# Sums of the two-level products and the last fold queued behind an older joining addition

## The chip, the cores and the metric

The kernel runs on one core of a Trainium2 chip. Its five engines run independently and wait for each other on semaphores: TensorE (PE in the profile, its weight loads PEld), VectorE (DVE), ScalarE (ACT), GpSimd (POOL) and SyncE (SP, which here issues most of the DMAs). The metric is the device time of one execution in microseconds; less is better. All data are float32.

## The reference

Two stages. The first is a sparse attention over q, k and v of shape (4, 8, 768, 64): each query sees the keys nearer than 16 positions and 24 block summaries (the maximum of a block's keys, the mean of its values). The second works on the result as x of shape (4, 768, 512):

```
X = np.fft.fft(x, axis=1); X = np.fft.fft(X, axis=2)
u = x + np.real(X)
un = (u - mean(u)) / np.sqrt(var(u) + 1e-6)          # over the last axis
out = u + np.maximum(un @ w_ch1, 0.0) @ w_ch2        # 512 -> 2048 -> 512
```

## The kernel before, in words

**Batches.** The four batches (b = 0 to 3) run as a software pipeline: while the two dense layers of batch b run on PE, the attention of batch b + 1 is put between them. The change lies in the third batch (b = 2, in the code `B - 2`) and in what of the fourth (`B - 1`) runs beside it.

**Dense layers.** The hidden layer has 2048 columns, cut into eight pairs of column blocks j = 0 to 7, four to a half (c = 0 and 1). Each layer is a Strassen-like product of seven multiplications in place of eight. `gen_hidden` makes the hidden values `h` of a half, `gen_out` the second layer. In `gen_out` a row-tile i (three of them) takes seven multiplications of four matmuls each (line 1829) into three banks (ox, oy, oz), and after each a *joining addition* on DVE adds a bank into `x` (`join`, line 1832; by `tt`, line 582): seven joins to a row-tile, 21 to a half. Each join sets `marks["dense"]`, so that this mark is always the newest join. `gen_out` yields four times to a row-tile, and at each yield calls `one_sum`, which for the first half of the third batch takes two groups of `early_sums`.

**Two-level products.** For the second half of the third batch the hidden layer is not made by `gen_hidden`, but by `gen_two`, which applies the scheme at two levels: two pairs of blocks, (4, 5) and (6, 7), with seven products each, and each of the 14 products (n = 0 to 13: "11", "U2", "11+", "U3", "Z", "12", "21", twice) of seven small matmuls on 192 columns (line 1691, numbered m = 1 to 7). Matmuls of three successive products interleave. ACT copies partial results between the banks t, f and g (line 1695), the matmuls add onto the copies, and DVE adds the finished parts into `h` (`add`, line 1648); these additions are chained one behind the other by `marks["turn"]`. `start_pairs` starts this generator just before the last multiplication of `gen_out`'s first half and fills the list `started`; `gen_pairs` then runs the rest, six matmuls to a yield.

**Sums.** The products need sums of the right operand (`first_sums`, of the columns of u) and of the left one (`pair_sums` for blocks 4 and 5, `left_halves`). Those are the twelve groups in `queue["early"]`, run by `early_sums` (line 1515). The left sums of the second pair of blocks, four groups in `queue["two"]`, are taken by `gen_two` itself, one after the matmul m = 3 of a product (line 1730). They come into the tiles named vw, uu, kt, left and w in the profile.

**Fold.** Ahead of the Fourier stage of a batch its rows and columns are folded (`fold_batch`: sums and differences of x with its mirrored half). For the last batch this runs at the end of `gen_attention(3)` in 22 steps: eight for each of two parities (`par`), then six for single tokens; POOL does the small copies, memsets and additions of single rows and columns. The mirrored rows come through memory by two DMAs of POOL (`turn_tiles`, lines 1041 and 1042). What the fold gives is first read by the `y` matmuls of `gen_fourier(3)` (line 1338).

**Order.** From here on the order on each engine is not written out by hand. A planner takes the instructions in the order of the program as priorities, and issues on each engine the first that is ready by its own estimate of durations; the order is then fixed. `tc.issue_after(ins)` adds that an instruction of the same engine may be issued only behind `ins`. The order of the program comes from `drive`, which advances two generators alternately: here 44 steps of `chain(gen_hidden(2, 0), gen_out(2, 0), gen_pairs(2))` to 80 steps of `gen_attention(3)`. A yield more or less in one generator therefore shifts its later steps against the other's.

Of the kernel before, what the change touches and what calls it, by code (L numbers as in the profile page):

```python
# [496 lines left out]
def _main_program(ctx, tc, q, k, v, moe_w_ch1, moe_w_ch2, out):  # L497
# [3 lines left out]
    B, H, S, D = q.shape  # L501
# [79 lines left out]
    def tt(out, in0, in1, op):  # L581
        return nc.vector.tensor_tensor(out=out, in0=in0, in1=in1, op=op).ins  # L582
# [5 lines left out]
    nat, marks = {}, {}  # L588

    def load(b, g, *which):  # L590

        for n in which or (1, 0):
            t = nat[b, g, n] = apool.tile([P, 2, NST // 2, 2 * D], FP, tag="nat", bufs=4, name=f"{'qk'[n]}n_{b}_{g}")
            if (b, g) > (2, 0):
                t = nat[b, g, n] = t.rearrange("p e j n -> p (e j n)").rearrange("p (m c) -> p m c", c=32)
                for e in range(2):
                    for h in range(2):
                        r, o = D * e + 32 * h, (q, k)[n][b, 2 * g + e].offset + 32 * h
                        fetch(out=t[r:r + 32], in_=bass.AP((q, k)[n].tensor, o, [[D, 32], [32 * D, S // 32], [1, 32]]))
                continue  # L600
            fetch(out=t.rearrange("p e j n -> p (e j) n"),
                  in_=(q, k)[n][b, 2 * g:2 * g + 2].rearrange("e (j p s) d -> p (e j) (s d)", p=P, s=2))
# [9 lines left out]
    def block_sums(b, gg):  # L612

        heads, rows = slice(4 * gg, 4 * gg + 4), 4 * nb
        f = BLOCK // 4
        n = f * D
        vb = spool.tile([rows, D], FP, tag="vbs", bufs=2, name=f"vbs_{b}_{gg}")
        for g in (2 * gg, 2 * gg + 1):
            sums[b, g] = vb, sel[:, g % 2]
        src = v[b, heads].rearrange("h (n f) d -> (h n) (f d)", f=BLOCK)  # L620
        if done_weights:
            raw = room(f"vb_{b}_{gg}")
            raw = [raw[0:rows, n * i:n * (i + 1)] for i in range(4)]
        else:

            raw = [bpool.tile([P, NC, P], FP, tag="s", bufs=5, name=f"vb_{b}_{gg}_{i}").rearrange("p n t -> p (n t)")
                   [0:rows] for i in range(4)]
        for i in range(4):
            fetch(out=raw[i], in_=src[:, n * i:n * (i + 1)])
        to_add[b, gg] = raw, vb  # L630
        if (b, gg) != (1, 0):
            add_later_blocks(b, gg)
# [23 lines left out]
    def load_values(b, g):  # L656
        if is_wide(b):
            load_wide_values(b, g)
            return
        load_narrow_values(b, g)  # L660
# [30 lines left out]
    def key_maxima(g):  # L691
        nc.vector.tensor_reduce(out=km_bufs[g % 2][:, 0:nb], in_=kt_bufs[g % 2][:, W:W + S].rearrange("p (n f) -> p n f", f=BLOCK),
                                op=ALU.max, axis=AX.X)
# [137 lines left out]
    def scale_sums(b, g):  # L831
        ps = abank([P, D], f"vs_{b}_{g}")
        vb, pick = sums[b, g]
        nc.tensor.matmul(ps, pick, vb, start=True, stop=True)
        for r in range(2):
            nc.scalar.activation(out=vs[:, r, 0:D], in_=ps, func=AF.Identity, scale=half_of[:, r:r + 1])
# [32 lines left out]
    def following(b, g, n):  # L869
        i = b * NP + g + n  # L870
        return divmod(i, NP) if i < B * NP else None
# [202 lines left out]
    def gen_attention(b):  # L1074
        x = bpool.tile([P, NST, DM], FP, tag="x", bufs=2, name=f"x_{b}")
        x_of[b] = x
        held = None
        if b == 2:
            load(2, 1)
            load(2, 2)  # L1080
        if b > 1:
            yield
            yield
            with tc.issue_after(marks["load"]):
                block_sums(b, 0)
            for _ in range(2):
                yield
        for g in range(NP + 1):
            n1, n3 = (following(b, g, n) for n in (1, 3))
            past = held  # L1090
            if (b, g) == (1, 1):
                with tc.issue_after(marks["mx", 0]):
                    key_maxima(g)
                held = scores(b, g)
            if past:
                if b > 1 and (b, g) != (B - 1, NP):
                    scale_sums(b, g - 1)
                values(b, g - 1, *past, x)
                if n1 and b > 1:
                    load_values(*n1)  # L1100
            if g == NP and b > 1:
                turn_tiles(b, x)
                if b == B - 1:
                    pair_sums(b - 1, 4)
                for _ in range(2 if b == B - 1 else 17):
                    yield
                rooms[b] = room(f"fold_{b}")
                steps = fold_batch(b, split_fold(b, rooms[b]))
                for n in range(99):
                    with tc.issue_after(marks["dense"]):  # L1110
                        done = next(steps, steps) is steps
                    if done:
                        break
                    yield
                    if b == B - 1 and n % 2:
                        yield
            elif held:
                for _ in range(5 if b > 1 else 1):
                    yield
            if (b, g) == (B - 1, NP - 1):  # L1120
                scale_sums(b, g)
                first_sums(b - 1)
            if g < NP:
                with tc.issue_after(marks["tile"]) if (b, g) == (1, 0) else ExitStack():
                    held = scores(b, g) if held is past else held
                sum_scores(b, g, held[1])
            if g and n1 and b == 1:
                load_values(*n1)
            if g == 1 and b > 1:
                block_sums(b, 1)  # L1130
            if g == NP and b > 1:
                return
            yield
            if g == NP:
                return
            for _ in range(2 if g == 0 and b > 1 else 0):
                yield
            if b == 1 and g < 2:
                for h in range(2):
                    with tc.issue_after(marks["sums", 0]) if g else ExitStack(), tc.high_priority(300) if g else ExitStack():  # L1140
                        (tt if g else gtt)(held[0][:, h], held[0][:, h], near[:, h], ALU.mult)
            if n1 and n1 != (1, 1):
                prepare(*n1, *((1,) if b > 1 else ()))
            if b == 1:
                scale_sums(b, g)
            if b > 1:
                yield
                yield
                if n1:
                    prepare(*n1, 0)  # L1150
            if n3 and not (b == 1 and n3 > (2, 0)):
                load(*n3)
            yield
            if b > 1:
                yield
# [357 lines left out]
    queue = {}  # L1513

    def early_sums():

        with tc.issue_after(marks["dense"]):
            for p in queue["early"].pop(0):
                tt(*p)

# [16 lines left out]
        rest[:] = [p[:, 9:12]]  # L1537
        queue["early"] += left_halves(b, j) + [*queue["third"]]

    rest, started = [], []  # L1540

    def start_pairs(b):

# [73 lines left out]
    def gen_two(b, c, pairs):  # L1617
# [107 lines left out]
        for k, (_, n, m) in enumerate(sorted(events, key=lambda e: e[0])):  # L1725
            if k == 1:
                h = wt["h", b] = bpool.tile([P, NC, 2, S], FP, tag="h", name=f"h_{b}_{c}")
            if n < N:
                step(n, m)
                if (n == 0 and m in (7, 3, 4, 5) if b == B - 1 else n > 1 and m == 3) and queue.get("two"):  # L1730
                    for part in queue["two"].pop(0):
                        add(*part)
            else:
                j, _, a, r = last
                i, kk = m
                if kk == 0:
                    ends[i] = bank([P, S2], f"hz_{b}_{c}_{i}")
                with tc.issue_after(marks["two"]):
                    marks["two"] = nc.tensor.matmul(ends[i], block(b, j + i, a, kk), u[:, r, kk, :], start=kk == 0,
                                                    stop=kk == 1, skip_group_check=True).ins  # L1740
                if kk:
                    v = view(j, 1, 0)[:, i]
                    add(v, ends[i], v, ADD)
                    nc.scalar.activation(out=v, in_=v, func=AF.Relu)  # L1744
            yield
# [38 lines left out]
    def gen_out(b, c):  # L1784
# [28 lines left out]
        for i in range(1 if plain else 0, HT):  # L1813
# [17 lines left out]

            def join(*a):
                marks["dense"] = tt(*a)
                if (b, c) == (B - 2, 1) and i:
                    joins.append(marks["dense"])

# [193 lines left out]
```

## Time and profile before

| | |
|---|---|
| median of 3 runs | 786.42 us (784.12 to 787.18) |
| profiled execution, its own time | 785.13 us |
| its span | 783.3 us |
| granted TensorE clock, mean | 0.995 |
| PE busy | 760.5 us (97% of the span) |
| DVE busy | 564.9 us (72%) |
| ACT busy | 268.7 us (34%) |
| POOL busy | 72.9 us (9%) |

The span is that of the recorded instructions of one execution; its own time also has the start and the end around them. A row of the timeline has the start in us from the beginning of the span, the busy time in us, the engine, the line of the code, the operation, what is written and read, the shapes and the number of like instructions run together. In square brackets stands how long the engine stood idle before it, and what ended that. A float32 matmul shows as two records.

### The profile page before, as it was taken

The page shows a single profiled execution, that of the slowest core. Times are in us where ns is not written, and L with a number is a line of the kernel's source. Part 1 is how long each engine was busy: PE and PEld are TensorE (multiplying, and loading weights), DVE is VectorE, ACT ScalarE, POOL GpSimd, SP SyncE. Part 2 cuts the span into 40 slices and gives each one's busy share as a digit, 9 for nine tenths or more (in the row PEclk, how much of TensorE's full clock was granted, in tenths as well). Part 3 has the DMA queues.
Part 4 walks back from the last instruction along what each step waited for, and adds up shares of the span by engine and source line. Part 5 has one row for each costly group of instructions (what it writes and reads, how often), then busy time and mean ns, then how long its engine had stood idle before and what let it go on. Part 6 is the DMA issues. An engine that isn't in the chain of part 4 may idle for free.

```text
span 783.3 us, 15327 instructions
## 1 busy us (share of the span) xinstructions
PE 760.5 (97%) x6152; PEld 596.3 (76%) x6152; DVE 564.9 (72%) x1197; ACT 268.7 (34%) x657; POOL 72.9 (9%) x102
## 2 busy tenths in 40 slices
PE   8998999999999999999999999999899999999996
PEld 5777654775598866787588856788889899889885
DVE  6799999998889454652859454659988987766751
ACT  5756656336626022100236022200466124104300
POOL 1001000000000022000310021100200005102400
PEclk9999999999999999999999999999999999999998
DMA  9997968797755299935541189610525153204001
GB/s 208 248 230 176 225 230 245 279 245 259 213 172 140 72 300 184 168 67 163 209 131 62 41 251 174 182 55 15 222 66 180 53 202 128 75 1 188 2 28 57
DMA packets 135904, 120.39 MB, mean 154 GB/s; under 512 B 94512, under 2 KB 117904, under 8 KB 135824
## 3 DMA queue, kind: packets, MB, share of 16 engines
q1 hardware_dynamic: 134672, 117.05, 54.1%
q0 software_dynamic: 576, 2.10, 0.8%
q8 instruction: 50, 0.82, 0.5%
q10 hardware_dynamic: 576, 0.17, 0.1%
q14 instruction: 30, 0.25, 0.1%
HBM read 97.28 MB, written 22.02 MB: 152 GB/s over the span
## 4 chain that ended last, share of the span: by engine, by line
PE 81%; DVE 11%; ACT 4%; issue 2%; DMA 1%; SPq 0%; DVEq 0%; ACTq 0%
PE ox L1829 18%; PE hx L1465 12%; PE oz L1829 9%; PE t L1691 6%; PE hz L1465 5%; PE oy L1829 4%; PE y L1338 3%; PE hy L1465 3%; PE f L1691 3%; PE sc L810 2%; DVE w L582 2%; DVE h L1648 2%; PE mx L1297 2%; PE av L846 2%; PE g L1691 1%
## 5 line engine op out<-in xcount | busy, mean ns | idle before, releaser
L1465 PE MATMUL hx<-u,w 128*128 128x384 f32 x320 | 117.0, 493 | 2.4 <-ACT h L1476 1.6
L1465 PEld LDWEIGHTS hx<-u,w 128*128 128x128 f32 x320 | 58.5, 190 | 46.0 <-ACT p L817 3.8
L1829 PE MATMUL oz<-w,s 128*128 128x256 f32 x368 | 89.0, 380 | 0.0
L1829 PE MATMUL ox<-w,s 128*128 128x256 f32 x368 | 88.0, 381 | 0.2 <-DVE x L582 0.2
L1829 PE MATMUL ox<-w,h 128*128 128x256 f32 x368 | 87.0, 380 | 0.1
L1829 PEld LDWEIGHTS ox<-w,h 128*128 128x128 f32 x368 | 69.1, 190 | 12.4 <-issue 1.7
L1829 PEld LDWEIGHTS ox<-w,s 128*128 128x128 f32 x368 | 68.7, 190 | 11.3 <-DVE x L582 1.1
L1829 PEld LDWEIGHTS oz<-w,s 128*128 128x128 f32 x368 | 69.4, 190 | 9.8 <-DVE x L582 0.6
L582 DVE TENSOR_TENSOR x<-ox,x 128x256 f32<-128x256 f32 x92 | 38.8, 421 | 44.7 <-PE ox L1829 44.4
L1695 ACT COPY f<-t 128x192 f32<-128x192 f32 x80 | 24.2, 303 | 119.3 <-PE t L1691 117.2
L1465 PE MATMUL hz<-u,w 128*128 128x384 f32 x160 | 58.8, 487 | 0.0
L1465 PEld LDWEIGHTS hz<-u,w 128*128 128x128 f32 x160 | 30.2, 190 | 20.8 <-ACT h L1483 0.4
L1829 PE MATMUL oy<-w,h 128*128 128x256 f32 x184 | 44.3, 380 | 0.7 <-ACT h L1744 0.7
L1829 PEld LDWEIGHTS oy<-w,h 128*128 128x128 f32 x184 | 34.7, 190 | 6.3 <-ACT h L1744 1.5
L1670 POOL TENSOR_SCALAR h<-h 128x768 f32<-128x768 f32 x12 | 25.4, 2129 | 143.8 <-DVE h L1648 143.8
L1648 DVE TENSOR_TENSOR h<-t,h 128x192 f32<-128x192 f32 (+1 forms) x80 | 30.6, 394 | 11.4 <-ACT f L1695 9.4
L582 DVE TENSOR_TENSOR x<-oz,x 128x256 f32<-128x256 f32 x46 | 19.4, 422 | 24.2 <-PE oz L1829 24.0
L1476 ACT COPY h<-hx 128x384 f32<-128x384 f32 x20 | 9.7, 483 | 78.9 <-PE hx L1465 78.9
L585 POOL TENSOR_TENSOR vb<-vb 96x512 f32<-96x512 f32 (+2 forms) x20 | 20.4, 1026 | 173.0 <-DVE h L582 65.5
L582 DVE TENSOR_TENSOR s<-h 128x512 f32<-128x512 f32 x46 | 31.3, 680 | 1.4 <-ACT h L1473 0.6
L1338 PE MATMUL y<-fs,fold 128*128 128x193 f32 x160 | 29.8, 329 | 0.6 <-ACT big L1344 0.3
L1465 PE MATMUL hy<-u,w 128*128 128x384 f32 x80 | 29.4, 488 | 0.0
(264 smaller groups left out, 1391.8 us busy)
## 6 DMA issues: line engine op xcount, KB each, us to landing
w<-dw SPq DMA_DIRECT2D x46, 896.0 KB, 6.1
words<-in_moe_w_ch_dram SPq DMA_DIRECT2D x32, 512.0 KB, 5.9
dw<-w SPq DMA_DIRECT2D x12, 896.0 KB, 7.3
vw<-in_v_dram SPq DMA_DIRECT2D x47, 192.0 KB, 5.8
out_dram<-x SPq DMA_DIRECT2D x23, 256.0 KB, 2.2
vb<-in_v_dram SPq DMA_DIRECT2D x24, 192.0 KB, 7.7
kn<-in_k_dram SPq DMA_DIRECT2D x9, 384.0 KB, 6.2
qn<-in_q_dram SPq DMA_DIRECT2D x9, 384.0 KB, 6.9
```

What stands on the lines that cost most here:

```text
L582: return nc.vector.tensor_tensor(out=out, in0=in0, in1=in1, op=op).ins
L585: return nc.gpsimd.tensor_tensor(out=out, in0=in0, in1=in1, op=op).ins
L810: ins = nc.tensor.matmul(ps[h][r:r + 64, i, :], kt[rows, o:o + 64], qt[rows, o:o + BLOCK], start=i == 0 or (b, g) != (B - 1, NP - 1), stop ...
L846: nc.tensor.matmul(av[r][32 * j:32 * (j + 1), t, :], p[rows, h, i - NB2 * h, :], vw[rows, i, :], start=(t == 0), stop=False, skip_group_ch ...
L1297: nc.tensor.matmul(out, y[:, g], table, start=False, stop=True, skip_group_check=True)
L1338: nc.tensor.matmul(y, fgs[b][par][:, st, P * g:P * (g + 1)], fs[par][:, g % 2, st, :], start=(st == 0), stop=(st == n - 1))
L1465: ins = nc.tensor.matmul(ps, w[:, a, kk, :], u[:, r, kk, :], start=start and kk == 0, stop=stop and kk == 1, skip_group_check=True)
L1648: marks["turn"] = f(**kw).ins
L1670: nc.gpsimd.tensor_scalar(out=t, in0=t, scalar1=0.0, scalar2=None, op0=ALU.max)
L1691: marks["two"] = nc.tensor.matmul(o, left(j, a, m), rhs(r, m), start=m in (1, 5), stop=m in (2, 3, 4, 5, 7), skip_group_check=True).ins
L1695: nc.scalar.copy(out={1: f[:, 0], 6: f[:, 1], 7: g}[m], in_=t)
L1829: nc.tensor.matmul(ps, left[a][:, n, :], wt[2, b, j][:, r, :], start=start and n == 0, stop=stop and n == NC - 1, skip_group_check=True)
```

## The change

Four edits, all in the order of instructions; no arithmetic is added or taken away.

1. `join` keeps the joins of the first half of the third batch in a list, `recent`.
2. `early_sums` are tied to the seventh-newest of these joins, in place of the newest.
3. The last batch's fold steps are tied to the seventh-newest join as long as the two-level products have not been started, and to the newest `marks["dense"]` after that, as before. The first twelve steps come two to a yield, the later ones with two yields after each; before, the yields after a step were one and two in turn.
4. The left sums of the second pair of blocks are taken from the fourth product of the third batch on (`n > 2`) in place of the third.

```diff
@@ gen_attention, the fold
                 for n in range(99):
-                    with tc.issue_after(marks["dense"]):
+                    with tc.issue_after(recent[-7] if b == B - 1 and not started else marks["dense"]):
                         done = next(steps, steps) is steps
                     if done:
                         break
-                    yield
-                    if b == B - 1 and n % 2:
+                    for _ in range(1 if b < B - 1 else n % 2 if n < 12 else 2):
                         yield
@@ early_sums
-        with tc.issue_after(marks["dense"]):
+        with tc.issue_after(recent[-7] if len(recent) > 6 else marks["dense"]):
             for p in queue["early"].pop(0):
                 tt(*p)
@@
-    rest, started = [], []
+    rest, started, recent = [], [], []
@@ gen_two
-                if (n == 0 and m in (7, 3, 4, 5) if b == B - 1 else n > 1 and m == 3) and queue.get("two"):
+                if (n == 0 and m in (7, 3, 4, 5) if b == B - 1 else n > 2 and m == 3) and queue.get("two"):
                     for part in queue["two"].pop(0):
                         add(*part)
@@ gen_out, join
                 marks["dense"] = tt(*a)
+                if (b, c) == (B - 2, 0):
+                    recent.append(marks["dense"])
```

## The prediction, made before the change was run

> **What bounds the kernel now.** I read first the page's busy times and the shares of the chain that ended last, to see which engine sets the time.
>
> ```profile
> PE 760.5 (97%) x6152; PEld 596.3 (76%) x6152; DVE 564.9 (72%) x1197; ACT 268.7 (34%) x657; POOL 72.9 (9%) x102
> ...
> PE 81%; DVE 11%; ACT 4%; issue 2%; DMA 1%; SPq 0%; DVEq 0%; ACTq 0%
> ```
>
> TensorE (PE) is busy 97% of the span and carries 81% of the chain, so a change of order gains only where PE stands still or waits between matmuls. I then cut the third batch's second layers and products into stretches by their busy times (columns: length, PE, weight loads, DVE, ACT, POOL, granted clock, DMA share, GB/s).
>
> ```profile
> core 0: us, PE busy (x) PEld busy (x) DVE busy (x) ACT busy (x) POOL busy (x), PEclk, DMA share, GB/s
> 515.00:530.00 15.00, 15.00 (x71) 13.09 (x71) 10.53 (x22) 0.00 (x0) 1.80 (x2) 1.00 0.21 71
> 530.00:545.00 15.00, 14.56 (x70) 12.56 (x69) 14.76 (x26) 0.91 (x3) 1.54 (x6) 1.00 0.00 0
> 545.00:549.70 4.70, 4.70 (x27) 4.44 (x26) 2.72 (x7) 1.71 (x5) 0.87 (x1) 1.00 0.54 181
> 549.70:577.00 27.30, 23.38 (x132) 20.76 (x131) 25.59 (x58) 14.11 (x43) 4.56 (x15) 1.00 0.39 147
> ```
>
> From 515 to 545 (the end of the first half's second layer) PE is full, except for 0.44 us. In 549.7 to 577 PE lacks 3.9 us of 27.3, while DVE is busy 25.6 of 27.3. In the stretches ahead DVE stands idle: 15 − 10.53 = 4.47, 15 − 14.76 = 0.24 and 4.70 − 2.72 = 1.98, together 6.7 us. So there is one place where DVE is the bound, and free DVE time just ahead of it.
>
> What PE loses is more than its idle time, since a matmul after a wait also runs longer. The rows of PE in that stretch:
>
> ```profile
> 540.78 0.59 PE L1691 MATMUL f<-u,w 128*128 128x192 f32 x2 [0.44 <-ACT f L1695]
> ...
> 547.13 0.49 PE L1691 MATMUL t<-vw,w 128*128 128x192 f32 x2
> ...
> 548.76 0.49 PE L1691 MATMUL t<-u,w 128*128 128x192 f32 x2
> ...
> 551.03 0.49 PE L1691 MATMUL t<-u,w 128*128 128x192 f32 x2
> ...
> 565.46 0.59 PE L1691 MATMUL g<-uu,w 128*128 128x192 f32 x2 [1.82 <-ACT g L1695]
> ...
> 583.31 0.59 PE L1829 MATMUL ox<-w,h 128*128 128x256 f32 x2
> ...
> 584.39 0.82 PE L1338 MATMUL y<-fs,fold 128*128 128x193 f32 x4
> ```
>
> The first matmuls of two successive products start at 548.76 and 551.03: 2.27 us for seven matmuls, 0.325 for one. The two-level products of line 1691 run as follows (same columns; the first is the third batch, the second the same products in the last batch):
>
> ```profile
> 546.92:584.39 37.47, 33.06 (x188) 30.35 (x188) 1.00 0.38 139
> 638.40:668.20 29.80, 28.70 (x174) 28.14 (x173) 1.00 0.50 193
> ```
>
> 188 records are 94 matmuls: 94 × 0.325 = 30.6 us. With the one inserted ox (583.31 to 583.74, 0.43) that is 31.0. From 547.13 to the first y at 584.39 they took 37.3. **The loss is 6.2 us.** In the last batch, where no fold runs beside the same products, 87 matmuls (28.3) stand in 29.8 us, of which two foreign ones take some 1.3: a loss of about 0.2. So the products can run nearly without gaps when DVE keeps up.
>
> Why DVE does not keep up, from its own rows in the order of time (the last number of a row with xN is the time of all N; 1029 and 582 are the fold's lines, 1648 the products' additions):
>
> ```profile
> 551.25 1.21 DVE L582 TENSOR_TENSOR fold<-x 128x1024 f32<-128x1024 f32 x1
> ...
> 553.57 0.68 DVE L582 TENSOR_TENSOR fold<-xr 128x512 f32<-128x512 f32 x1
> ...
> 554.63 1.15 DVE L1648 TENSOR_TENSOR left<-w 128x512 f32<-128x512 f32 x2
> ...
> 556.83 0.95 DVE L582 TENSOR_TENSOR fold<-fold 128x768 f32<-128x768 f32 x1
> ...
> 560.36 1.00 DVE L1648 TENSOR_TENSOR h<-t,h 128x192 f32<-128x192 f32 x3
> ...
> 562.35 1.01 DVE L582 TENSOR_TENSOR fold<-fold 128x381 f32<-128x381 f32 x2
> ...
> 564.24 0.36 DVE L1648 TENSOR_TENSOR zs<-t,zs 128x192 f32<-128x192 f32 x1 [0.62 <-ACT zs L1712]
> 564.52 0.55 DVE L1648 TENSOR_TENSOR h<-f,h 128x384 f32<-128x384 f32 x1
> ...
> 566.78 1.49 DVE L1648 TENSOR_TENSOR h<-h,zs 128x768 f32<-128x768 f32 x1
> ...
> 569.17 0.96 DVE L1648 TENSOR_TENSOR h<-h,zs 128x768 f32<-128x768 f32 x1
> ...
> 571.24 0.94 DVE L1648 TENSOR_TENSOR h<-t,h 128x384 f32<-128x384 f32 x2
> ...
> 575.42 0.41 DVE L582 TENSOR_TENSOR fold<-fold 128x256 f32<-128x256 f32 x1
> ```
>
> The fold's second parity (fold<-x at 551.25, its mirrored rest, two of 0.95 of which the first is at 556.83, and the first of the two at 562.35) stands between the additions that free the accumulators. The addition h<-f at 564.52 is of a product whose matmul ended near 560; ACT's copy waits for it, and PE for the copy, which is the 1.82 us at 565.46:
>
> ```profile
> 565.10 0.30 ACT L1695 COPY g<-t 128x192 f32<-128x192 f32 x1 [0.89 <-DVE h L1648]
> ```
>
> The fold's operations in this stretch, all together:
>
> ```profile
> 549.70:577.00 27.30, 0.00 (x0) 0.00 (x0) 7.47 (x12) 0.00 (x0) 4.56 (x15) 1.00 0.39 147
> ```
>
> 7.47 us of DVE in 12 groups of records.
>
> **The change, part by part.**
>
> *Sums tied to the seventh-newest join (line 1517).* Twelve groups of sums for the products are moved, nothing is added. Each is now queued directly behind the newest of the joining additions of the second layer; the next join stands behind it.
>
> ```profile
> 516.90 0.42 DVE L582 TENSOR_TENSOR x<-ox,x 128x256 f32<-128x256 f32 x1
> ...
> 520.20 0.42 DVE L582 TENSOR_TENSOR x<-ox,x 128x256 f32<-128x256 f32 x1 [1.57 <-PE ox L1829]
> ...
> 522.79 0.42 DVE L582 TENSOR_TENSOR x<-ox,x 128x256 f32<-128x256 f32 x1 [0.64 <-PE ox L1829]
> 524.52 0.42 DVE L582 TENSOR_TENSOR x<-oy,x 128x256 f32<-128x256 f32 x1 [1.30 <-PE oy L1829]
> 524.86 1.62 DVE L582 TENSOR_TENSOR vw<-u 128x768 f32<-128x768 f32 x2
> ...
> 534.71 0.95 DVE L582 TENSOR_TENSOR kt<-left,w 128x768 f32<-128x768 f32 x1
> ...
> 535.78 1.22 DVE L582 TENSOR_TENSOR fold<-x 128x1024 f32<-128x1024 f32 x1
> ```
>
> Now DVE waits 1.57, 0.64 and 1.30 us for PE ahead of three joins (520.20, 522.79, 524.52), and only then may the first two sums (1.62) start. With the tie seven joins back they may fill those waits: the join that the first sums would then follow (seven joins to a row-tile, two more made when they are queued: the third of the row-tile before) ended by 517.3 (the row at 516.90). By the code their inputs are made or fetched in earlier stages (the batch's normalised input, the weights of blocks 4 and 5). They issue no DMA, and SP's queue is not passed. What waits behind them: a join delayed by one sum in progress. The largest single one is 0.95 (kt<-left, 534.71); 0.95 + 0.42 for the join is 1.37 us, and between two products into the same bank PE has another product's 1.73 (522.79 to 524.52). So one sum costs nothing; two in a row cost 2 × 0.95 + 0.42 − 1.73 = 0.6 us for each join. Ends: −0.44 (the only gap there is) to +0.6 for each join hit. I take 0, because the early joins have waits of 0.6 to 1.6 ahead of them and later ones had sums directly before them already, with PE full.
>
> *The fold's steps (lines 1107 to 1116).* Of 22 steps the first twelve now come two to a yield, the later ones two yields apart, and until the products have been started they are tied to the seventh-newest join. By the interleaving (44 steps of the products' generator to 80 of attention) steps 0 to 12 will fall ahead of the last join of this layer; now steps 0 to 5 do, 6 and 7 follow at once. Moved are the second parity's first five operations: 1.21 + 0.68 + 0.95 + 0.95 + 0.55 = 4.34 us (0.68 for 512 columns as in fold<-xr, 0.55 as half of the pair at 562.35 with its overlap). They must fit into the 6.7 us of DVE idle, which they do. The first fold operation ran at 535.78 and may now run from the mid 520s; the second needs the mirrored rows:
>
> ```profile
> 519.50 1.05 POOL L1042 DMA_INDIRECT xr<-turned,mirror  x1 [3.25 <-DMA turned<-x]
> ...
> 566.75 0.71 POOL L585 TENSOR_TENSOR fold<-fold 1x256 f32<-1x256 f32 x1 [5.87 <-DVE fold L582]
> ```
>
> ```profile
> DMA to landing us min/median/max: 4.4/4.4/4.5
> ```
>
> Issued at 519.50 and 4.4 us to land, they are there at 524: no wait. The small POOL copies and adds of the fold follow their DVE steps, on a POOL queue with nothing else in it here; the steps issue no DMA. What remains beside the products is 7.47 − 4.34 = 3.1 us (three fold steps and four additions of 0.41 like that at 575.42), and these come up earlier in the order, tied to the products' own additions. Ends: all 6.2 us come back, or none, if the left sums keep DVE behind (next part).
>
> *Left sums of the second pair one product later (line 1730).* Four groups of 1.15 (554.63, 564.98 are the first and last) now follow products 3 to 6 (counted from 0) in place of 2 to 5. The last is read by product 7's matmul f<-u,left, which comes 2.27 + 3 × 0.325 = 3.25 us after that product's first. Without gaps that product starts at 548.76 + 5 × 2.27 = 560.1, so it wants the sum at 563.4. Product 2's last matmul would end at 551.03 + 2.27 + 0.33 + 0.49 = 554.1, its last additions take 0.94 (as at 571.24), so DVE is free at 555. Before the last sum ends it has: 0.55 + 0.36 + 1.00 for product 3, 0.36 + 0.36 for product 4, 0.55 + 0.36 + 0.94 + 0.96 + 0.96 for product 5, 0.55 for product 6 and 4 × 1.15: 11.5 us in records. Records overlap by 0.08 a step (three of 0.36 take 1.00, two of 0.55 take 1.01), over some 15 steps 1.2, which leaves 10.3; 0.4 more for the copy that product 4 waits for. It ends at 555 + 10.7 = 565.7, so PE stops for about 2.3 us, and 0.4 goes into the longer first matmuls. With the sums left one product earlier, the bound by the same count would be the addition h<-f of product 6, done at about 565.2, whose bank product 8 wants at 563.7: 1.5 us. So this edit alone costs 0.8 here, or down to −0.5 if the first sum, at 554.63 now, would have had DVE wait for its weights; I take 0.8.
>
> *Sum.* 6.2 lost now, 2.7 left: 3.5 us back. The copy gap of 0.44 at 540.78 belongs to starting the products and stays. The profiled execution's 785.13 becomes 781.6; it lies 1.29 below the median of 786.42, so the median becomes **782.9 us**. What is late next is product 7's left sum.
>
> One thing speaks against the gain: POOL. h<-h at 566.78 took 1.49 where the same addition at 569.17 is one of 0.96, and POOL added at 566.75 for 0.71: 0.53 us on DVE. At 571.24, with POOL adding as well, two additions out of PSUM took the usual 0.94. The fold's two single-row additions of the second parity come some 13 us earlier now and meet the left sums, whose operands are all in SBUF: up to 2 × 0.53 = 1.1 us of the gain; this is rival P. [...]
>
> **The rivals.**
>
> *A, forecast (0.37): part of the loss returns.* Gain 2.4 to 4.8, time 781.6 to 784.0.
>
> *P (0.10): POOL's adds meet the left sums.* As worked out above: 3.5 − 1.1 = 2.4 back, 784.0. For it speaks 1.49 against 0.96; against it that the POOL adds take 0.71 each and DVE has waits early in the stretch.
>
> *B (0.25): the stretch runs as in the last batch.* For it speaks the loss of 0.2 there, and that the scheduler may set the remaining fold steps into waits of DVE. Against it: there the left sums stand before the products, not among them. Gain 6.2 − 0.8 = 5.4, 781.0; with the 0.44 too, at most 6.6, 779.8.
>
> *C (0.17): nothing comes back.* The fold leaves the stretch, but the left sums, now behind products 5 and 6 where DVE's 3.77 already exceeds a product's 2.27, with four token additions (4 × 0.41 = 1.6 in records) and POOL's 1.1 put ahead of the last sum: 2.7 + 1.6 + 1.1 = 5.4 of 6.2. Time 784.9 to 787. The change would then not do what it is there to do.
>
> *D (0.11), slower: the joins wait.* With DVE full from 517 on, the order is fixed ahead, and a join set behind two sums or fold steps costs PE 0.6 us. With seven joins to a row-tile there are a dozen after 522. Six of them cancel 3.5 us; all twelve cost 7.2: 786.4 − 3.5 + 7.2 = 790.1. Against it: PE can take another product's matmuls first, as it did with the products' first matmuls around 540.78.
>
> **How the numbers follow.** 0.5% of 786.4, about what a measurement can tell from no change, is 3.9 us. Faster by more: all of B and 0.17 of A's upper end, 0.42. Within: the other 0.20 of A, P and C, 0.47. Slower: D, 0.11. The range holds A, P, most of B and C to the present median: 780.0 to 786.9.
>
> **What would show it.** First sums on DVE (vw<-u) near 518 in place of 524.86, and DVE's waits of 1.57 and 1.30 gone; the second fold<-x ahead of 547 in place of 551.25; PE's idle between 549.7 and 577 below 2 us, with the 1.82 at 565 gone and one stop of about 2 us, if any, ahead of f<-u,left of product 7; PE without waits from 515 to 545. The prediction is wrong if PE shows new waits for x ahead of ox or oz, if the second parity still runs after 550, or if the four left sums keep the stretch as long as now.

## The result, and the profile after

| | before | after |
|---|---|---|
| median | 785.78 us (784.12 to 787.18, 6 runs) | 781.54 us (779.45 to 781.98, 6 runs) |
| ratio | | 0.9941, 95% interval 0.9922 to 0.9959 |
| profiled execution, its span | 785.13 us, 783.3 us | 779.45 us, 777.6 us |

The changed kernel is 4.2 us (0.59%) faster; 782.9 had been forecast, and the interval of the gain (0.41% to 0.78%) lies across the 0.5% that parted "faster" from "same". Below, lines have moved: 1691, 1695, 1829, 1338, 1648 and 1998 of before are 1690, 1694, 1828, 1337, 1647 and 1999 of after.

The page's lines of the span, of busy time and of the chain that ended last, after:

```profile
span 777.6 us, 15332 instructions
...
PE 759.5 (98%) x6152; PEld 597.0 (77%) x6152; DVE 563.8 (73%) x1197; ACT 268.9 (35%) x657; POOL 75.3 (10%) x102
...
PE 78%; DVE 15%; ACT 4%; issue 2%; DMA 1%; SPq 0%; DVEq 0%
```

The amount of work has not changed, and PE remains the bound. The busy times by stretch, after (same columns and limits as before):

```profile
515.00:530.00 15.00, 15.00 (x70) 12.92 (x69) 14.99 (x26) 0.00 (x0) 2.23 (x2) 1.00 0.21 66
530.00:545.00 15.00, 14.98 (x71) 12.82 (x69) 15.00 (x29) 0.56 (x2) 6.04 (x17) 1.00 0.12 37
545.00:549.70 4.70, 4.63 (x29) 4.60 (x29) 2.28 (x6) 2.92 (x11) 1.02 (x2) 1.00 0.94 343
549.70:577.00 27.30, 24.58 (x141) 24.29 (x140) 22.49 (x57) 16.29 (x48) 1.02 (x2) 0.94 0.27 99
```

DVE is now full from 515 to 545 (14.99 and 15.00 where 10.53 and 14.76 stood) and PE is full there too. In the products DVE fell from 25.59 to 22.49 and PE lacks 2.72 instead of 3.92 us. But PE's granted clock in that stretch is 0.94, where it was 1.00. One caution: the whole schedule of this execution runs 2.0 us earlier than before's, for a reason far ahead of this place (below). In stretches moved by 2.0 us DVE's four figures are 14.89, 15.00, 2.79 and 22.30, and PE's idle time is the same, so the reading holds.

The fold's own operations in the products' stretch, and DVE's rows in the order of time, after:

```profile
549.70:577.00 27.30, 0.00 (x0) 0.00 (x0) 1.82 (x5) 0.00 (x0) 1.02 (x2) 0.94 0.27 99
```

```profile
515.24 1.22 DVE L582 TENSOR_TENSOR fold<-x 128x1024 f32<-128x1024 f32 x1
...
517.31 1.62 DVE L582 TENSOR_TENSOR vw<-u 128x768 f32<-128x768 f32 x2
...
539.86 1.21 DVE L582 TENSOR_TENSOR fold<-x 128x1024 f32<-128x1024 f32 x1
...
541.93 1.81 DVE L582 TENSOR_TENSOR fold<-fold 128x768 f32<-128x768 f32 x2
...
560.41 0.95 DVE L1647 TENSOR_TENSOR h<-h,zs 128x768 f32<-128x768 f32 x1
...
563.13 0.55 DVE L1647 TENSOR_TENSOR h<-f,h 128x384 f32<-128x384 f32 x1
563.60 1.15 DVE L1647 TENSOR_TENSOR left<-w,left 128x512 f32<-128x512 f32 x2
```

The sums start 7.5 us earlier and the fold's second parity 11.4 us earlier (5.6 and 9.4 without the 2.0 us of the whole schedule), and 1.82 us of fold are left beside the products, of 7.47 (2.20 in the moved stretch). Where the old kernel had seven waits of PE in this stage, one is left:

```profile
564.34 0.59 PE L1690 MATMUL f<-u,left 128*128 128x192 f32 x2 [2.72 <-DVE left L1647]
...
565.90 0.85 PE L1690 MATMUL g<-uu,w 128*128 128x192 f32 x2
566.54 0.85 PE L1690 MATMUL t<-u,w 128*128 128x192 f32 x2
...
568.39 0.49 PE L1690 MATMUL f<-u,left 128*128 128x192 f32 x2
...
580.86 0.82 PE L1337 MATMUL y<-fs,fold 128*128 128x193 f32 x4
```

It is the stop that the prediction named, on the matmul that it named. Behind it something follows that it did not name: matmuls 0.64 us apart (565.90 to 566.54) instead of 0.325. PE alone, in stretches around the stop (length, PE busy, granted clock, DMA share, GB/s):

```profile
557.00:561.40 4.40, 4.40 (x29) 1.00 0.30 90
561.60:564.30 2.70, 0.01 (x1) 1.00 0.52 146
564.90:568.30 3.40, 3.40 (x13) 0.50 0.00 0
568.40:572.00 3.60, 3.60 (x24) 1.00 0.00 0
```

For 3.4 us behind the stop PE ran at clock 0.50 and did 13 records where e_after3 below does 21 in as long: 8 records of 0.16 us, about 1.3 us lost.

**Where the 5.7 us between the two profiled executions lie.** The order of instructions differs only between the third batch's second layer and the end of its products, so a time from a fixed point ahead of it to one behind it is comparable. I take the last attention values (line 851) before it and the first y after it, and call that *the stage*. Its start before and after:

```profile
512.97 0.94 PE L851 MATMUL av<-vs,p 64*128 64x130 f32 x12
```

```profile
510.98 0.94 PE L851 MATMUL av<-vs,p 64*128 64x130 f32 x12
```

Before: 584.39 − 512.97 = 71.42 us. After: 580.86 − 510.98 = 69.88. The stage gave back **1.54 us**, not 3.5. A second piece lies far ahead of the stage, which itself starts 1.99 us earlier (512.97, 510.98). Most of it is PE's wait at one place where it waits for no other engine (before, then after):

```profile
75.75 1.03 PE L846 MATMUL av<-vw,p 64*32 64x65 f32 x53 [2.50 <-issue]
```

```profile
74.26 0.84 PE L846 MATMUL av<-vw,p 64*32 64x65 f32 x53 [0.82 <-issue]
```

It makes 2.50 − 0.82 = 1.68 us. Across the traces of this study it ran from 0.8 to 3.5 us, and two (e_sums_at_2b and p_pace) do not have it, with the same order of instructions on PE there; it is scatter. And it draws more behind it: in all eleven traces where it is 1.95 us or longer, PE's granted clock is 0.50 for 3.4 or 6.8 us after it (in before from 75.98 to 79.39), and in after, with 0.82, it stays at 1.00. The third piece is at the end, DVE's own queue behind the last output, in the views of the two lines (name, count, shortest/median/longest ns, first to last start); before, then after:

```profile
L1998 DVEq COMPARE_BRANCH  x1: 72/72/72, 777.1 to 777.1; - x1
L1998 DVEq EVENT_SEMAPHORE  x1: 21/21/21, 780.0 to 780.0; - x1
...
L2025 DVEq DRAIN  x2: 10/72/135, 782.4 to 782.8; - x2
```

```profile
L1999 DVEq COMPARE_BRANCH  x1: 72/72/72, 773.5 to 773.5; - x1
L1999 DVEq EVENT_SEMAPHORE  x1: 21/21/21, 776.5 to 776.5; - x1
...
L2026 DVEq DRAIN  x2: 10/14/17, 776.7 to 777.1; - x2
```

From DVE's last branch to the end of the span it was 6.2 us (777.1 to 783.3) and is 4.1 (773.5 to 777.6), some 2.2 us less by the unrounded times. The three pieces, 1.99, 1.54 and 2.2, make up the 5.7. Before, DVE's drain stood 2.4 us behind the instruction ahead of it; after, 0.2. No edit touches this place. So the measured gain was near the forecast, but made of other terms, and the experiments had three questions: what each edit is worth, whether the slow matmuls belong to the stop, and what shortened the tail.

### The profile page after: what moved, and what is told of

Same layout as the page of the kernel before. It is cut to its first block, busy times and chain, and to the rows that moved or that the text cites. A ratio compares the mean times of both kernels' runs of the same rounds, so it can differ in the third digit from the quotient of the medians.

```text
span 777.6 us, 15332 instructions
## 1 busy us (share of the span) xinstructions
PE 759.5 (98%) x6152; PEld 597.0 (77%) x6152; DVE 563.8 (73%) x1197; ACT 268.9 (35%) x657; POOL 75.3 (10%) x102
## 4 chain that ended last, share of the span: by engine, by line
PE 78%; DVE 15%; ACT 4%; issue 2%; DMA 1%; SPq 0%; DVEq 0%
PE ox L1828 18%; PE hx L1464 11%; PE oz L1828 9%; PE t L1690 6%; PE hz L1464 5%; PE oy L1828 5%; PE y L1337 3%; PE f L1690 3%; DVE w L582 3%; PE hy L1464 3%; PE mx L1296 2%; PE sc L810 2%; PE g L1690 2%; DVE w L1203 1%; DVE words L1201 1%
```

## The experiments

Stage as defined above, *tail* from DVE's last branch to the end of the span, both from the trace; medians with the number of runs. The medians of before beside them were 785.72 us (18 runs) for e_before2, e_after2, e_sums_at_2 and e_fill, 787.02 (one run) for the four named p_, and 785.52 (14 runs) for the other four.

| kernel | median us | ratio to before | stage | tail | half clock behind PE's stop |
|---|---|---|---|---|---|
| before | 785.78 (6) | – | 71.42 | 6.27 | no |
| e_before2 | 786.85 (1) | – | 71.44 | 6.48 | no |
| after | 781.54 (6) | 0.9941 [0.9922, 0.9959] | 69.88 | 4.10 | 3.4 us |
| e_after2 | 779.38 (5) | 0.9916 [0.9886, 0.9945] | 69.96 | 4.10 | 3.4 us |
| e_after3 | 781.13 (6) | 0.9934 [0.9918, 0.9950] | 68.44 | 4.07 | no |
| e_sums_at_2 | 778.16 (6) | 0.9901 [0.9870, 0.9931] | 67.21 | 4.10 | no stop |
| e_sums_at_2b | 778.72 (6) | 0.9904 [0.9888, 0.9920] | 67.21 | 4.26 | no stop |
| e_fill | 782.40 (12) | 0.9962 [0.9943, 0.9982] | 70.61 | 4.12 | no |
| p_sums | 784.05 (1) | – | 70.42 | 5.67 | no |
| p_fold | 779.25 (1) | – | 69.00 | 4.10 | no |
| p_pace | 784.75 (1) | – | 71.37 | 4.10 | 3.4 us |
| p_late | 787.66 (1) | – | 74.78 | 6.43 | 6.8 us |
| b_pad1 | 782.86 (6) | 0.9956 [0.9940, 0.9973] | 71.42 | 4.10 | no |
| a_minus1 | 783.51 (9) | 0.9966 [0.9952, 0.9979] | 68.79 | 6.29 | no |

**The two kernels again.** e_before2 is before unedited, e_after2 and e_after3 are after unedited: how far do traces of the same kernel agree?

> The kernel before, once more, for a second trace of it. Theory 1 (the stage of the change makes the difference): from the last row-tile of the first half to the first y of the last batch it takes 68.7 us again, with the 1.82 us wait at product 6, and the rows outside that stage are like those of the changed kernel within their own scatter. Theory 2 (a part of the measured 4.2 us comes from elsewhere): the 2.5 us wait of PE near 73 us, which the changed kernel's trace does not have, and the 2 us longer tail behind the last matmul are here again.

> The changed kernel, once more. Theory 1: ratio 0.992 to 0.996; PE stops 2.7 us ahead of product 7's f<-u,left again, since DVE ends that sum late in a fixed order; the half clock behind it comes again only if it depends on the stop. Theory 2: the stage is again only 1.5 us shorter than before and the rest of the gain lies ahead of it or behind it.

> The changed kernel, for comparison on the same chip. Stage 69.9, tail 4.1, the 2.7 us stop again. If the stage's 1.5 and the tail's 2.3 are all: ratio 0.994 to 0.996.

The stage of before repeats within 0.02 us (71.42, 71.44; 71.42 in b_pad1, which has the same order there). That of after does not: 69.88 and 69.96, but 68.44 in e_after3, with the same stop:

```profile
567.78 0.59 PE L1690 MATMUL f<-u,left 128*128 128x192 f32 x2 [2.72 <-DVE left L1647]
```

PE alone around it, in e_after3:

```profile
565.00:567.70 2.70, 0.06 (x1) 1.00 0.51 146
568.30:571.70 3.40, 3.40 (x21) 1.00 0.00 0
```

Clock 1.00 and 21 records in 3.4 us. So the half clock is not a fixed consequence of the stop, and it accounts for the 1.4 to 1.5 us between the two lengths of the stage. In the five traces with a stop of 2.7 to 2.85 us ahead of these matmuls (after, e_after2, e_after3, a_minus1, e_fill) two have it and three not.

The traces show what parts the two from the three. In them the granted clock changes on a grid: in e_after2 it is 0.50 from 76.68 to 83.51 and again from 568.20 to 571.61, and these times lie 2, 142 and 1 times 3.413 us apart; in before it is 0.50 from 75.98 to 79.39 and again from 779.12, 1 and 205 times 3.413 us. Where such a half clock stands early in a trace, it gives the grid for the rest. The interval of the grid in which the stop begins, and the next one, in after and then in e_after3:

```profile
561.49:564.90 3.41, 0.69 (x4) 1.00 0.41 116
564.90:568.32 3.42, 3.42 (x13) 0.50 0.00 0
```

```profile
563.57:566.98 3.41, 1.49 (x10) 1.00 0.40 117
566.98:570.39 3.41, 2.61 (x16) 1.00 0.00 0
```

In after the whole stop (561.62 to 564.34) lies in one interval, in which PE is busy for 0.69 us; in e_after3 a border of the grid cuts it into 1.92 and 0.80. The seven stops of 2.3 us and more in this stage all fit: the most idle time in one interval is 2.72 (after), 2.73 (e_after2), 2.36 (p_pace) and 2.54 (p_late) where the half clock follows, and 1.92 (e_after3), 1.63 (a_minus1) and 1.46 (e_fill) where it does not. No run moves the stop against the grid on purpose, so this is seven of seven, and no experiment. Nor is idle time the whole measure: at the wait near 75 us, among smaller matmuls, 1.8 us in one interval were enough in e_after3, where PE waits from 73.69 to 75.77 and a border of the grid lies at 75.46, 143 intervals ahead of 563.57.

**The last edit taken back: e_sums_at_2, and once more as e_sums_at_2b.**

```diff
-                if (n == 0 and ... if b == B - 1 else n > 2 and m == 3) and queue.get("two"):
+                if (n == 0 and ... if b == B - 1 else n > 1 and m == 3) and queue.get("two"):
```

> The change without its last edit: the second pair's left sums again from the third product on. Theory 1 (the last sum is what is late): the 2.7 us stop ahead of f<-u,left goes, a smaller one of about 1.5 comes at product 8's copy, no half clock; 1 to 2.5 us faster than the changed kernel, 779 to 780.5. Rival (the edit is needed, because at the third product DVE waits for the weights or is not free): a stop as long or longer earlier, 781.5 to 783.5.

> The change without its last edit, on the same chip as the changed kernel. If the stage's 4.2 (67.2 against 71.4) and the tail's 2.3 are all: ratio 0.991 to 0.993, 2 to 3 us faster than the changed kernel.

All of PE's waits in the stage of e_sums_at_2:

```profile
562.77 0.59 PE L1690 MATMUL g<-uu,w 128*128 128x192 f32 x2 [0.31 <-ACT g L1694]
...
565.56 0.59 PE L1690 MATMUL g<-uu,w 128*128 128x192 f32 x2 [0.21 <-ACT g L1694]
```

The stop is gone and 0.52 us of waits are left, in the chain of DVE's addition, ACT's copy and PE's g that made the 1.82 before; the prediction had counted a stop of 1.5 without this edit. The stage takes 67.21 both times: 1.2 less than after without half clock, 2.7 less than after with it. By medians, each beside after on the same chip, it is 1.2 (779.38 to 778.16) and 2.4 us (781.13 to 778.72); the intervals of the ratios overlap both times, so it is the stage that shows the difference. This is the fastest of the versions that were run more than once, 0.990 of before.

**Filling the stop: e_fill.** Seven matmuls whose result nothing reads, set directly ahead of the waiting one.

```diff
+            if b < B - 1 and (n, m) == (7, 3):
+                for _ in range(7):
+                    with tc.issue_after(marks["two"]):
+                        marks["two"] = nc.tensor.matmul(z, left(j, a, 1), rhs(r, 1), start=True, stop=True, ...).ins
```

> The changed kernel with seven extra matmuls of 192 columns into an unused part of product 7's bank just ahead of f<-u,left, 2.3 us of work that nothing reads. Theory 1 (the stop lets the clock fall, and the half clock costs 1.6 us more): no half clock behind the stop, matmuls stay at 0.33 us, 1 to 2 us faster than the changed kernel in its stage. Rival (the half clock is chance, not due to the stop): it is there in some runs of both, no difference, or up to 0.5 slower.

```profile
566.01 2.54 PE L1691 MATMUL t<-u,w 128*128 128x192 f32 x14 [2.85 <-ACT g L1698]
```

The stop did not fill: the first filler itself waited 2.85 us, for an ACT copy of the bank that it writes, and then the 14 records of the seven took 2.54 us more. The expected gain did not come: the stage takes 70.61, which is e_after3's 68.44 and the fillers' time. There is no half clock behind the stop in this trace, but the grid cuts this stop into 1.39 and 1.46, and by the other six none was to be expected even without fillers. The experiment is inconclusive: whether an active PE at this place would keep the clock up stays untested.

**Each edit alone, on before.** p_sums has `recent` and the tie of `early_sums`; p_fold the tie of the fold and its new yields; p_pace the new yields alone; p_late `n > 2` alone.

```diff
@@ p_sums
-        with tc.issue_after(marks["dense"]):
+        with tc.issue_after(recent[-7] if len(recent) > 6 else marks["dense"]):
@@ p_fold
-                    with tc.issue_after(marks["dense"]):
+                    with tc.issue_after(recent[-7] if b == B - 1 and not started else marks["dense"]):
@@ p_fold and p_pace
-                    yield
-                    if b == B - 1 and n % 2:
+                    for _ in range(1 if b < B - 1 else n % 2 if n < 12 else 2):
                         yield
@@ p_late
-                if (n == 0 and ... if b == B - 1 else n > 1 and m == 3) and queue.get("two"):
+                if (n == 0 and ... if b == B - 1 else n > 2 and m == 3) and queue.get("two"):
```

> The kernel before with the first edit alone (the sums tied to the seventh-newest join). Stage from the last av of the last batch's attention to the first y: 71.4 us before, 69.9 changed, 67.2 without the last edit. Theory 1 (what counts is DVE time moved ahead of the products): the 4 us of DVE idle ahead are used, so the second parity of the fold moves ahead by some 4 us, but stays tied to the newest additions: 69 to 70.5. Rival (the sums alone only move idle time, since the fold stays behind the products' additions): 71 to 71.5.

> The kernel before with the fold's tie and its new pace, the sums as before. Theory 1: DVE is nearly full from 530 to 545 as before, but the fold's steps have priority ahead of the joins of the third row-tile: part of the second parity still falls among the products, 68.5 to 70.5, and joins come later, with a wait or two of PE for x. Rival (the sums' tie is not needed, the fold's own is enough): 67.2 to 67.8.

> The kernel before with only the new pace of the fold's steps (two to a yield), all ties as before. Theory 1: the steps come earlier in the order, but DVE has no free time for them before 545: 69.5 to 71.5. Rival (the pace alone does it): 67.2 to 68.5.

> The kernel before with the last edit alone (the left sums one product later). Theory 1 (the edit makes the last sum late): a wait for the left sum ahead of product 7's f<-u,left of 2.5 us or more, in place of the 1.82 us wait, 72 to 74.5 against 71.4. Rival (with the fold still among the products the later sums help the additions that free the banks): 69.5 to 71.

One run each, so I read the stage, not the time. Against 71.42: sums −1.0, fold −2.4, pace −0.05, late +3.4. The waits that tell why, first of p_sums, whose 1.82 ahead of g is that of before (gone are the 0.44 ahead of the products and two of about 0.3 among them):

```profile
565.42 0.59 PE L1690 MATMUL g<-uu,w 128*128 128x192 f32 x2 [1.82 <-ACT g L1694]
```

p_fold, where a join comes late on DVE, which had waited for the mirrored rows and then had fold steps and two sums to do; DVE's row, then PE's:

```profile
522.64 0.69 DVE L582 TENSOR_TENSOR fold<-xr 128x512 f32<-128x512 f32 x1 [1.72 <-DMA xr<-turned,mirror]
```

```profile
528.26 1.99 PE L1828 MATMUL ox<-w,s 128*128 128x256 f32 x8 [1.40 <-DVE x L582]
```

p_pace, where the faster fold steps still queue behind the newest join:

```profile
546.12 3.67 PE L1828 MATMUL ox<-w,s 128*128 128x256 f32 x8 [2.36 <-DVE x L582]
```

and p_late, where the fold is still among the products and the left sums come later still (the wait of 1.82 stays, and 6.8 us at half clock follow, which is part of the +3.4):

```profile
569.40 1.01 PE L1691 MATMUL f<-u,left 128*128 128x192 f32 x2 [4.23 <-DVE left L1648]
```

In p_pace the 1.82 and the other fold waits of the products are gone, and one late join with a half clock behind it took all of it back: this is the mechanism of rival D, and the older tie is what keeps it out of the change. Both ties together (e_sums_at_2) give −4.2, more than −1.0 and −2.4, since the waits of 1.40 and 0.44 in p_fold are gone: with sums to do early, DVE comes to the mirrored rows only at 528.9 and does not wait for them.

**The tail: b_pad1 and a_minus1.** In the traces, DVE's instruction stream has 1408 instructions in before, waits included, and 1409 in after: one wait on a semaphore more. Theory: the count alone moves the tail. b_pad1 is before with a memset of one value given twice, a_minus1 is after with that memset on POOL.

```diff
@@ b_pad1, on before
             nc.vector.memset(all_ok[:, 1:2], 1.0)
+            nc.vector.memset(all_ok[:, 1:2], 1.0)
@@ a_minus1, on after
-            nc.vector.memset(all_ok[:, 1:2], 1.0)
+            nc.gpsimd.memset(all_ok[:, 1:2], 1.0)
```

> The kernel before with one more instruction on DVE (a second memset of one column, where DVE is free). Theory T (the tail behind the last matmul hangs on DVE's number of instructions: 1408 in the kernel before, 1409 in the changed one, and the last of its code is fetched separately when the count is 1408 or less): DVE's drain follows its first instruction behind the branch at once, not 2.3 us later; the tail behind the branch is 4.1 us in place of 6.3 to 6.5, the ratio 0.9965 to 0.9978, the stage stays 71.4. Rival (the tail is shorter because of the order in the changed kernel): tail 6.3, ratio 1.000.

> The changed kernel with one instruction fewer on DVE (that memset on POOL). Theory T: 1408 instructions, DVE's drain 2.3 us late, tail 6.3; stage 69.9 as in the changed kernel; 2 to 2.5 us slower than the changed kernel, ratio to before 0.996 to 0.999. Rival: tail 4.1, ratio as the changed kernel's.

The lines of the tail in b_pad1, then in a_minus1:

```profile
L1999 DVEq EVENT_SEMAPHORE  x1: 21/21/21, 780.5 to 780.5; - x1
...
L2026 DVEq DRAIN  x2: 10/14/17, 780.6 to 781.1; - x2
```

```profile
L1999 DVEq EVENT_SEMAPHORE  x1: 21/21/21, 777.7 to 777.7; - x1
...
L2026 DVEq DRAIN  x2: 10/72/135, 780.0 to 780.5; - x2
```

One instruction more on the old kernel: its drain follows at once, and the kernel is 2.66 us faster (785.52 to 782.86) with the stage at 71.42 as ever. One instruction less on the changed kernel: 2.3 us between the two again, and 783.51 against 781.13. So 2.2 us of the change's gain have nothing to do with the products. All traces agree: the tail is 6.27 to 6.48 us in the four with 1408 instructions and 4.07 to 4.26 in the nine with 1409, p_pace among them, whose stage is as long as before's. What p_sums adds, with 1407 instructions: there the drain follows the first instruction at once, and a gap of 2.2 us stands one instruction later (DVE's semaphore at 781.8, its drain at 779.6).

```profile
L2026 DVEq DRAIN  x2: 17/18/18, 779.6 to 781.9; - x2
L2026 DVEq EVENT_SEMAPHORE  x2: 21/21/21, 781.8 to 782.1; - x2
```

The gap moves by one instruction with the count by one: it is bound to a place in DVE's program. One more thing in the traces goes with it: the page's line of the queue of the kind "instruction", in before, then in after.

```profile
q14 instruction: 30, 0.25, 0.1%
```

```profile
q14 instruction: 29, 0.24, 0.1%
```

It counts 30 packets in before, a_minus1 and p_late, with 1408 instructions on DVE, and 29 in after, e_after2, e_after3, e_sums_at_2, e_fill and b_pad1, with 1409. In before one packet of this queue (0.01 MB, at 780.6) is all that the DMA queues move from 779.0 to 782.3, and it lies in the gap; in after they move nothing from 775.4 to 777.0. Whether DVE waits in the gap for that packet is not shown: p_sums has its gap with 29 packets. From DVE's branch to its next instruction it is 3.0 to 3.2 us with and without the gap (777.1 to 780.0 before, 773.5 to 776.5 after, 773.1 to 776.3 in e_sums_at_2b).

## Why the prediction was right or wrong

**The place and the mechanism: right.** The second fold<-x was to run ahead of 547 (539.86), the first sums near 518 (517.31), PE to have no waits from 515 to 545 (none), and the 1.82 was to go (gone). The 6.7 us of free DVE time were taken up: in the three stretches up to 549.7 DVE now stands idle for 2.4 us (4.70 − 2.28), all of it behind 545. The sums' price of 0 held. The fold went further than expected: its first fold<-x ran at 515.24, not from the mid 520s.

**The stop ahead of product 7's left sum: right in place, a little small in size.** 2.3 us of idle time were forecast, and 2.72 measured. That the whole pair of sums must end first was not so: PE starts at 564.34, the pair ends at 564.75. The sign "PE idle in 549.7 to 577 below 2 us" was set too low beside the prediction's own 2.3, and failed: 27.30 − 24.58 = 2.72.

**What the stage gives back, 3.5: over-sized.** The traces say 1.5 with the half clock and 2.6 to 3.0 without it (a_minus1 68.79, e_after3 68.44). By medians the change without the shorter tail is a_minus1 against before, 2.0 us, and e_after3 against b_pad1, both with the short tail, 1.7. The failing term is the 2.7 that was to be left. By the prediction's own count, 97 product matmuls at 0.325 and one ox at 0.43 make 31.96 us; from the first of them behind the last run of ox to the first y it took 35.53 in e_after3 (547.34 to 582.87) and 36.97 in after (543.89 to 580.86). So 3.6 us are lost without the half clock: 2.72 of idle time and 0.85 in matmuls that start late, where 2.3 and 0.4 had been counted (before loses 6.3 by the same count). With the half clock 5.0 are lost: the stop was priced by its own length, and the clock that halves behind it costs up to 1.4 more. Intervals of the 3.413 us grid with 2.36 to 2.73 us of idle time were enough for the half clock (p_pace, p_late, after, e_after2), though PE was busy for the rest of them; 1.92 us and less were not (e_after3, a_minus1, e_fill). The 0.44 ahead of the products, which was to stay, went too.

**The last edit, 0.8: mis-sized.** 1.2 to 2.7 in the stage. Without the edit PE waits 0.52 where a stop of 1.5 had been counted, so the count of DVE's work from product 2's end was too long for that case (with the matmuls that start late, the products of e_sums_at_2 lose 2.3 us: 546.04 to 580.33, less 31.96); with the edit the stop is longer than counted, and the risk of the half clock comes with it. The edit alone, on the old kernel, costs even 3.4.

**The sum: near for the wrong reason.** It assumed that nothing outside the stage moves. The stage gave back less than forecast, and a shorter tail that no term had made up for it: that is luck. Stage 1.5 to 3.0 and tail 2.2 make 3.7 to 5.2; measured were 4.2, 6.3 and 4.4 (after, e_after2, e_after3; the interval of the second, 4.3 to 9.0 us, reaches into that range). Without the tail the change would have stood at about 784, still within the range.

**The rivals.** P did not come. POOL's additions of the second parity, after:

```profile
545.94 0.71 POOL L585 TENSOR_TENSOR fold<-fold 1x256 f32<-1x256 f32 x1 [1.06 <-DVE fold L582]
...
549.94 0.72 POOL L585 TENSOR_TENSOR fold<-fold 1x256 f32<-1x256 f32 x1 [2.92 <-DVE fold L1029]
```

Both are over before the first left sum (553.62), and h<-h,zs at 560.41 takes 0.95 where it took 1.49: the fold's move took this meeting away. (The first parity's two now meet sums: vw<-u at 537.59 and 538.99 take 1.15 and 0.94, 0.2 us each above their like, and PE does not wait.) B (the stretch runs as in the last batch) did not come: even e_sums_at_2 loses 2.3 us where the last batch was counted at 0.2. C was wrong; of D, late joins showed only in single edits on the old kernel (p_pace 2.36 us, p_fold 1.40).

## What to carry to other kernels

A stop of the bound engine is not priced by its length alone: behind stops of 2.36 to 2.85 us TensorE ran 3.4 us at half clock in three of six traces here (after, e_after2 and p_pace; not e_after3, a_minus1 and e_fill), and in all six it went with where the stop lay on a grid of 3.41 us. That risk belongs into the price, one trace does not show it, and an edit that leaves one long stop is worth a run without it. Work is well moved into an engine's free time when its tie is loosened together with its order: the faster fold steps alone gained nothing, with the older tie 2.4 us and with the sums moved as well 4.2. And before a gain of some 0.3% is put down to an edit, compare the time between two fixed points around it and look at the end of the program: one instruction more or less on DVE moved the total by as much here.

## What was not expected of the hardware

- One more instruction on DVE ahead of its last branch took 2.2 us off the end of the execution, whether it was a wait on a semaphore (after) or a memset (b_pad1); one less put them back (a_minus1).
- Behind a stop of 2.36 to 2.73 us TensorE's granted clock was 0.50 for 3.4 us: in two of five traces with the stop of after, and in p_pace. The 4.23 us of p_late had 6.8 us of it. In all seven it followed when 2.36 us or more of the stop lay in one interval of the 3.41 us grid, and did not at 1.92 or less.
- PE's wait for "issue" near 75 us, with nothing else late, ran from 0.8 to 3.5 us in twelve traces and was missing in two, whatever the kernel, and from 1.95 us on it had 3.4 or 6.8 us at half clock behind it. Its cause stays open.
